# A ninth token block written to the two halves of one set of columns, and scaled on GpSimd with the even blocks

## The chip, the cores and the metric

The kernel runs on one core of a Trainium2 chip: TensorE (PE, with its weight loads PEld), VectorE (DVE), ScalarE (ACT), GpSimd (POOL), SyncE (SP, which issues DMAs), and DMA engines. The metric is the device time of one execution in microseconds (us), lower is better. Three runs of the kernel before gave 999.74, 1000.41 and 995.54 us, median 999.74.

## The reference

Attention with a threshold, and behind it a mixture of experts that sends each token to one expert. Cut to what is computed:

```python
# q, k, v: (8 sequences, 8 heads, 576 tokens, 64) f32
scores = scale * q @ k.T
scores = where(scores >= max(scores) - tau, scores, -1e9)
attn = exp(scores - max(scores)); attn /= sum(attn) + 1e-9
x = (attn @ v), heads side by side            # (4608 tokens, 512)
logits = x @ w_gate; e = argmax(logits)       # 8 experts
gate = softmax(logits)[e]; eom = sigmoid(x @ w_output_gate)[e]
out = gate * eom * (relu(x @ w1[e]) @ w2[e])  # w1: 512 x 1024, w2: 1024 x 512
```

## The kernel before

**Units.** Two sequences are worked on together, one in the partitions 0 to 63, one in 64 to 127. A unit is one head of such a pair: 4 pairs x 8 heads = 32 units. A sequence of 576 tokens is four blocks of 128 tokens and a rest of 64; with two sequences that is nine blocks of 128 rows, the ninth holding the 64 last tokens of both.

**Steps.** `Attention.run` goes through the units in five steps each (t = 0 to 4), with one order written out by hand for PE, DVE, ACT and POOL. In a step PE computes the scores of block t (L128) into PSUM tiles ps, DVE reduces them to their least negative (L137, tile s), POOL makes the threshold from that (thr, L142), ACT takes the exponential (L149), and in the next step DVE applies the mask and sums (L159). Two steps after the scores PE transposes the block: the remainder, 64 keys, in L177 into the banks pr and pa, the rest in L190 into pt; ACT copies both out into PTa and PTb (L181 and L192). pt is one buffer: L190 of the next step writes it again only when ACT has copied it. Attention times v (L221) of the unit before runs in between, and leaves X, 64 features of each sequence by 576 tokens.

**x_rows and what follows it.** In step 4 `x_rows` (L243 to L252) turns X of the unit before into rows of tokens, and gives the logits with them: wx is an identity of 64 columns beside 16 gate columns, so each matmul gives 80 columns. Sequence 0 goes to the bank pr, sequence 1 to pa, five blocks each. A matmul in f32 is two passes, so there are ten passes for each sequence. ACT copies pa and pr to xl (L314), with the remainder's copies (L181) in between, since they share the banks. Then `x_out` scales by the reciprocal of the sums: POOL the blocks of 128 tokens (L262), ACT the ninth block, one half from each sequence (L264). POOL scales the logits (L271). Behind that, in step 0 of the next unit, ACT copies pt to PTb (L192).

**Ninth block in before.** The fifth matmul of both sequences is 128 columns wide: sequence 0 takes its tokens from 512 and 64 columns of zeros, sequence 1 its tokens from 448, so that the last 64 land in the lower half. Each sequence has its own columns in xl, reciprocals and logits (10 of them), and the router copies the lower half of the logits of sequence 1 into one common block (L483).

**Router and experts.** After eight units the logits of a pair are summed (L282), routed and the rows scattered to DRAM by POOL (L456); the expert stage, from about 519 us on, is matmuls of 128 rows and 128 columns (L928 to L952), with weights loaded by SP and split on ACT and DVE.

Of the kernel before, what the change touches and what calls it, by code (L numbers as in the profile page):

```python
# [8 lines left out]
F32 = mybir.dt.float32  # L9
# [3 lines left out]
AF = mybir.ActivationFunctionType  # L13
ALU = mybir.AluOpType
AX = mybir.AxisListType
PSUM = bass.MemoryType.PSUM
P = 128
# [4 lines left out]
class Attention:  # L22
# [9 lines left out]
    def __init__(self, ctx, tc, ident, qkv, tau, wg, shape, router):  # L32
        self.tc, self.nc = tc, tc.nc
        nc = self.nc
        self.qkv = qkv
        self.B, self.H, self.S, self.D = shape
        self.NB = self.S // P
        self.M = self.NB * P
        self.R = self.S - self.M
        self.HS = self.S // 2  # L40
        self.KP = self.S + self.R
        self.QA = 2 * P
        self.NK = 2 * self.NB + 1
        self.nu = self.B // 2 * self.H
        self.router = router
        pool = lambda name, bufs, **kw: ctx.enter_context(tc.tile_pool(name=name, bufs=bufs, **kw))
        self.ld = pool("ald", self.LB)
        self.sp = pool("asp", 3)
        self.const = pool("aconst", 1)
        self.vld = pool("avld", self.VB)  # L50
        self.w2 = pool("aw2", 1)
        self.w3 = pool("aw3", 3)
        self.xp = pool("axp", 1)
        self.ps_s = pool("ps_s", 2, space=PSUM)
        self.ps_t = pool("ps_t", 1, space=PSUM)
        self.ps_a = pool("ps_a", 1, space=PSUM)
        self.ps_r = pool("ps_r", 1, space=PSUM)
        c = self.const
        self.ident = ident
        self.tau = c.tile([P, 1], F32, name="tau_sb")  # L60
        self.tau_in, self.wg_in = tau, wg
        warm = c.tile([P, 1], F32, name="warm")
        nc.vector.memset(warm, 0.0)
        nc.scalar.activation(warm, warm, AF.Exp)
        E2 = wg.shape[2]
        self.XW = self.D + E2
        self.wx = c.tile([P, self.H, self.XW], F32, name="wx")
        self.X = [c.tile([P, self.S + 64], F32, name=f"X{i}") for i in range(2)]
        self.half = [slice(0, 64), slice(64, P)]
        for pp in self.half:  # L70
            nc.gpsimd.tensor_copy(
                self.wx[pp, :, 0 : self.D], ident[pp, None, pp].broadcast_to([self.D, self.H, self.D])
            )
        for x in self.X:
            nc.gpsimd.memset(x[0:64, self.S :], 0.0)
        self.loaded, self.sums, self.rinv, self.lt, self.sumup = {}, {}, {}, {}, None

    def load_qk(self, u, first=False):
# [73 lines left out]
    def masks(self, u, t, ss, mn, thr, p, between=None):  # L152
        nc, S = self.nc, self.S
        if t == 0:
            self.sums[u] = self.w3.tile([P, 10], F32, name="sums")
        sums = self.sums[u]
        for a, s in enumerate(ss):
            e = p[:, a * S : a * S + S]
            nc.vector.scalar_tensor_tensor(  # L159
                e, s, thr[:, a : a + 1], e, op0=ALU.is_le, op1=ALU.mult, accum_out=sums[:, 2 * t + a : 2 * t + a + 1]  # L160
            )
            if a == 0 and between:
                between()
# [61 lines left out]
                yield (lambda: nc.scalar.copy(X[:, q0 : q0 + N], pa[:, 0:N])) if i == self.NB else None  # L225

    def denominators(self, u):
        r = self.rinv[u] = self.w3.tile([P, 10], F32, name="rinv")
        s = self.sums.pop(u)
        self.nc.gpsimd.tensor_scalar(r[:, 0:9], s[:, 0:9], 1e-9, None, op0=ALU.add)  # L230
        self.nc.gpsimd.tensor_copy(r[:, 9:10], r[:, 8:9])

    def inverse(self, u):
        r = self.rinv[u]
# [8 lines left out]
    def x_rows(self, u):  # L243
        X, pp, W, h = self.X[u % 2], self.half, self.XW, u % self.H
        ps = [pool.tile([P, 512], F32, name=name) for pool, name in ((self.ps_r, "pr"), (self.ps_a, "pa"))]
        for j in range(self.NB + 1):
            for a in range(2):
                c0 = self.M - 64 * a if j == self.NB else j * P
                self.nc.tensor.matmul(
                    ps[a][:, j * W : j * W + W], X[pp[a], c0 : c0 + P], self.wx[pp[a], h], start=True, stop=True  # L250
                )
        return ps  # L252

    def x_out(self, u, xl):
        nc, r, pp, D = self.nc, self.rinv[u], self.half, self.D
        bp, h = divmod(u, self.H)
        R = self.rows(bp)
        hs = slice(h * D, h * D + D)
        ra = r.rearrange("p (j a) -> p a j", a=2)
        for a in (1, 0):  # L260
            o = R[:, 0:8, hs].rearrange("p (j a) d -> p a j d", a=2)[:, a]
            nc.gpsimd.tensor_tensor(o, xl[:, a, 0:4, 0:D], ra[:, a, 0:4, None].broadcast_to([P, 4, D]), op=ALU.mult)  # L262
        for a in (1, 0):
            nc.scalar.activation(R[pp[a], 8, hs], xl[pp[a], a, 4, 0:D], AF.Copy, scale=r[pp[a], 8:9])  # L264

    def logits(self, u, xl):
        rt, r, E2 = self.router, self.rinv.pop(u), self.XW - self.D
        bp, h = divmod(u, self.H)
        if h == 0:
            self.lt[bp] = rt.small.tile([P, 10, E2, self.H], F32, name="ltx")  # L270
        self.nc.gpsimd.tensor_tensor(  # L271
            self.lt[bp][:, :, :, h].rearrange("p (j a) c -> p a j c", a=2), xl[:, :, :, self.D :],
            r.rearrange("p (j a) -> p a j", a=2)[:, :, :, None].broadcast_to([P, 2, 5, E2]), op=ALU.mult,
        )
        if h == self.H - 1:
            self.sumup = bp, rt.small.tile([P, 10, E2], F32, name="LX", bufs=2)

    def logit_sums(self, k):
        rt = self.router
        bp, LX = self.sumup  # L280
        ks = slice((0, 3, 6, 8)[k], (3, 6, 8, 10)[k])
        self.nc.vector.tensor_reduce(LX[:, ks], self.lt[bp][:, ks], axis=AX.X, op=ALU.add)  # L282
        if k == 3:
            self.lt.pop(bp)
            self.sumup = None
            rt.queue.append(rt.route(bp, rt.xrows[bp], LX))

    def run(self, hooks):
        nc, T, nu, rt = self.nc, self.NB + 1, self.nu, self.router
        G, W = nu * T, self.XW  # L290
        st, pr, av = {}, {}, {}
        self.prep_first()
        for g in range(G + T):
            u, t = divmod(g, T)
# [7 lines left out]
            if g < G:  # L302
                ps = [self.ps_s.tile([P, 1024], F32, name="ps") for _ in range(1 if t == self.NB and u else 2)]
# [3 lines left out]
            if xu is not None:  # L307
                px = self.x_rows(xu)
                out = self.remainder(t2, pr[g2], px) if rem else None
                if g < G:  # L310
                    pr[g] = self.exps(u, t, *st[g])
                xl = self.w2.tile([P, 2, 5, W], F32, name="xl")
                for a in (1, 0):
                    nc.scalar.copy(xl[:, a].rearrange("p j w -> p (j w)"), px[a][:, 0 : 5 * W])  # L314
                    if out:
                        out(a)
                self.x_out(xu, xl)
            elif g < G:
                pr[g] = self.exps(u, t, *st[g])
# [8 lines left out]
            if rem and xu is None:  # L328
                if not u:
                    self.pa = self.ps_a.tile([P, 512], F32, name="pa")  # L330
                out = self.remainder(t2, pr[g2], (self.ps_r.tile([P, 512], F32, name="pr"), self.pa), bool(u))
# [29 lines left out]
class Router:  # L361
# [109 lines left out]
    def route(self, bp, rows, LX):  # L471
        nc, E = self.nc, self.E
# [6 lines left out]
        cand, oh, t1, d = (t3(x) for x in ("cand", "oh", "t1", "d"))  # L479
        ohb = t3("ohb", BF16)  # L480
        V = nc.vector
        yield False
        nc.scalar.copy(LX[64:P, 8], LX[64:P, 9])  # L483
        yield True
        l, og = LX[:, 0:n, 0:E], LX[:, 0:n, E:]
        V.tensor_reduce(mx, l, axis=AX.X, op=ALU.max)
# [183 lines left out]
class Experts:  # L670
# [17 lines left out]
    def pool(self, name, bufs, **kw):  # L688
        return self.ctx.enter_context(self.tc.tile_pool(name=name, bufs=bufs, reuse_waits="tile", **kw))
# [460 lines left out]
```

## Time and profile before

| what | value |
|---|---|
| median of three runs | 999.74 us |
| the profiled execution, its own time | 1000.44 us |
| its span from first to last instruction | 998.4 us |
| PE busy | 963.6 us (97%) |
| DVE busy | 672.6 us (67%) |
| ACT busy | 631.6 us (63%) |
| POOL busy | 326.0 us (33%) |
| attention stage | to about 519 us |

The busy share of PE counts modelled ends of pipelined matmuls, so a short wait of PE can be partly hidden in it; from the start of one group of instructions to the start of the next nothing is hidden. Shapes such as 64*128 in a row of PE are the rows and columns of the array that the instruction uses.

### The profile page before, as it was taken

The page shows a single profiled execution, that of the slowest core. Times are in us where ns is not written, and L with a number is a line of the kernel's source. Part 1 is how long each engine was busy: PE and PEld are TensorE (multiplying, and loading weights), DVE is VectorE, ACT ScalarE, POOL GpSimd, SP SyncE. Part 2 cuts the span into 40 slices and gives each one's busy share as a digit, 9 for nine tenths or more (in the row PEclk, how much of TensorE's full clock was granted, in tenths as well). Part 3 has the DMA queues.
Part 4 walks back from the last instruction along what each step waited for, and adds up shares of the span by engine and source line. Part 5 has one row for each costly group of instructions (what it writes and reads, how often), then busy time and mean ns, then how long its engine had stood idle before and what let it go on. Part 6 is the DMA issues. An engine that isn't in the chain of part 4 may idle for free. (4 is left out here: it accounts for less than half of the span.)

```text
span 998.4 us, 21641 instructions
## 1 busy us (share of the span) xinstructions
PE 963.6 (97%) x8201; PEld 694.0 (70%) x8201; DVE 672.6 (67%) x1607; ACT 631.6 (63%) x1249; POOL 326.0 (33%) x617
## 2 busy tenths in 40 slices
PE   8999999999999999999989989999999999999994
PEld 4656566665666656666558878788878878878783
DVE  7888889888898888988865754435535535536621
ACT  6898888888889898898983333324424424425510
POOL 4344343458434584356625402012002102002101
PEclk9999999999999999999999999999999999999997
DMA  9972122123212233122227854345626426537301
GB/s 272 260 257 81 41 80 60 62 81 126 91 55 67 80 127 91 43 79 94 76 76 241 235 171 148 113 137 167 212 83 231 163 91 224 161 129 238 108 0 43
DMA packets 68841, 127.16 MB, mean 127 GB/s; under 512 B 6143, under 2 KB 32895, under 8 KB 68736
## 3 DMA queue, kind: packets, MB, share of 16 engines
q1 hardware_dynamic: 62096, 104.75, 33.7%
q0 software_dynamic: 6640, 21.02, 5.6%
q8 instruction: 65, 1.06, 0.4%
q14 instruction: 40, 0.33, 0.1%
HBM read 96.31 MB, written 30.22 MB: 127 GB/s over the span
## 5 line engine op out<-in xcount | busy, mean ns | idle before, releaser
L137 DVE TENSOR_SCALAR_CACHE_REDUCE s<-ps 128x576 f32<-128x576 f32 x288 | 207.4, 753 | 69.6 <-PE ps L128 68.8
L149 ACT ACTIVATE p<-s,mn 128x576 f32<-128x576 f32 x288 | 210.6, 774 | 60.4 <-DVE s L137 58.9
L159 DVE SCALAR_TENSOR_TENSOR p<-s,thr,p 128x576 f32<-128x576 f32 x288 | 224.9, 814 | 0.0
L128 PE MATMUL ps<-qk 64*128 64x288 f32 (+1 forms) x1152 | 194.4, 419 | 0.0
L142 POOL TENSOR_SCALAR thr<-mn,tau_sb 128x2 f32<-128x2 f32 (+1 forms) x160 | 117.5, 734 | 227.1 <-DVE s L137 224.8
L933 ACT ACTIVATE hh<-ph 128x512 fp32r<-128x512 f32 (+2 forms) x96 | 48.9, 510 | 208.1 <-PE ph L930 200.0
L934 DVE SCALAR_TENSOR_TENSOR hl<-ph,hh 128x512 fp32r<-128x512 f32 (+2 forms) x96 | 55.4, 577 | 142.7 <-ACT hh L933 142.6
L928 PE MATMUL ph<-xh,w1h 128*128 128x512 f32 (+2 forms) x384 | 136.5, 356 | 0.9 <-ACT xl L314 0.9
L929 PE MATMUL ph<-xl,w1h 128*128 128x512 f32 (+2 forms) x384 | 133.9, 349 | 0.2 <-DVE xl L755 0.2
L930 PE MATMUL ph<-xh,w1l 128*128 128x512 f32 (+2 forms) x384 | 133.7, 348 | 0.0
L128 PEld LDWEIGHTS ps<-qk 64*128 64x128 f32 (+1 forms) x1152 | 111.6, 189 | 21.2 <-DVE s L137 1.9
L952 PE MATMUL py<-w2h,hl 128*128 128x512 f32 x304 | 120.9, 398 | 4.5 <-DVE hl L934 4.5
L743 POOL DMA_INDIRECT out_dram<-yo,kid x39 | 44.0, 1129 | 236.8 <-DVE yo L742 87.6
L950 PE MATMUL py<-w2h,hh 128*128 128x512 f32 x304 | 120.3, 396 | 1.0 <-ACT hh L933 1.0
L951 PE MATMUL py<-w2l,hh 128*128 128x512 f32 x304 | 120.2, 395 | 0.0
L221 PE MATMUL pa<-PTb,vld 128*64 128x320 f32 x640 | 102.1, 447 | 0.7 <-ACT PTb L206 0.7
L190 PE MATMUL pt<-ident,p 64*128 64x64 f32 x2048 | 86.6, 224 | 8.1 <-ACT PTb L192 7.9
L221 PE MATMUL pa<-PTa,vld 128*64 128x256 f32 x640 | 83.2, 389 | 0.8 <-ACT PTb L181 0.8
L190 PEld LDWEIGHTS pt<-ident,p 64*128 64x128 f32 x2048 | 74.1, 139 | 12.6 <-ACT PTb L192 12.2
L755 DVE TENSOR_TENSOR w1l<-r,w1h 128x1024 fp32r<-128x1024 f32 x52 | 63.6, 1223 | 26.2 <-ACT w1h L752 25.3
L928 PEld LDWEIGHTS ph<-xh,w1h 128*128 128x128 f32 x384 | 72.6, 189 | 12.2 <-ACT xl L314 1.1
L929 PEld LDWEIGHTS ph<-xl,w1h 128*128 128x128 f32 x384 | 72.7, 189 | 10.2 <-DVE xl L755 0.6
(201 smaller groups left out, 1515.8 us busy)
## 6 DMA issues: line engine op xcount, KB each, us to landing
r<-in_moe_w_dram SPq DMA_DIRECT2D x104, 512.0 KB, 3.9
qk<-in_qkv_dram SPq DMA_DIRECT2D x31, 640.0 KB, 4.0
vld<-in_qkv_dram SPq DMA_DIRECT2D x32, 320.0 KB
xs<-zrow SPq DMA_DIRECT2D x32, 257.0 KB, 8.8
xg<-xs SPq DMA_DIRECT2D x6, 1028.0 KB, 5.3
xg<-xs SPq DMA_DIRECT2D x4, 514.0 KB
xg<-xs SPq DMA_DIRECT2D x2, 771.0 KB
out_dram<-yo,kid POOLq DMA_INDIRECT x39
```

The source lines that it names most:

```text
L128: nc.tensor.matmul(ps[a][:, c0 + hf * HS : c0 + hf * HS + HS], qs[pp], k[pp, k0 + hf * HS : k0 + hf * HS + HS], start=True, stop=True,)
L137: nc.vector.tensor_scalar(s, ps[a][:, c0 : c0 + S], SC, None, op0=ALU.mult, op1=ALU.min, accum_out=mn[:, a : a + 1])
L149: self.nc.scalar.activation(e, s, AF.Exp, bias=mn[:, a : a + 1], scale=-1.0)
L159: nc.vector.scalar_tensor_tensor(e, s, thr[:, a : a + 1], e, op0=ALU.is_le, op1=ALU.mult, accum_out=sums[:, 2 * t + a : 2 * t + a + 1])
L190: nc.tensor.transpose(pt[:, o : o + 64], p[hs[h], k0 : k0 + P], id_[hs[h], hs[h]])
L221: nc.tensor.matmul(pa[self.half[a], 0:N], vm[:, kb, a], PT[:, 4 * a + kb if i else self.NK - 1], start=(i == 0), stop=(i == self.NB), skip ...
L928: nc.tensor.matmul(ph, w1h[:, c, fs], self.xh[:, c, 0:N], start=(c == 0), stop=False)
L929: nc.tensor.matmul(ph, w1h[:, c, fs], self.xl[:, c, 0:N], start=False, stop=False)
L930: nc.tensor.matmul(ph, w1l[:, c, fs], self.xh[:, c, 0:N], start=False, stop=(c == 3))
L950: nc.tensor.matmul(Y, hh[:, ts], wh, start=(f == 0), stop=False)
L951: nc.tensor.matmul(Y, hh[:, ts], wl, start=False, stop=False)
L952: nc.tensor.matmul(Y, hl[:, ts], wh, start=False, stop=(f == 7))
```

## The change

The ninth block's two matmuls take 64 columns of X each as the stationary side, and write the two halves of the partitions of one set of 80 columns, both in pr. So xl, the reciprocals, the logits and their sums have nine blocks instead of ten in two groups; pa is copied with four blocks and pr with five, into every second place of xl. POOL scales the even blocks, now with the ninth, and the odd blocks; the two scaled copies on ACT, the copy of the ninth reciprocal on POOL, the copy in the router and the zero columns of X are gone.

```diff
-        self.X = [c.tile([P, self.S + 64], F32, name=f"X{i}") for i in range(2)]
+        self.X = [c.tile([P, self.S], F32, name=f"X{i}") for i in range(2)]
...
-        for x in self.X:
-            nc.gpsimd.memset(x[0:64, self.S :], 0.0)
...
-        self.nc.gpsimd.tensor_scalar(r[:, 0:9], s[:, 0:9], 1e-9, None, op0=ALU.add)
-        self.nc.gpsimd.tensor_copy(r[:, 9:10], r[:, 8:9])
+        self.nc.gpsimd.tensor_scalar(r, s, 1e-9, None, op0=ALU.add)
...
-                c0 = self.M - 64 * a if j == self.NB else j * P
+                last = j == self.NB
+                out = ps[0][pp[a], j * W : j * W + W] if last else ps[a][:, j * W : j * W + W]
                 self.nc.tensor.matmul(
-                    ps[a][:, j * W : j * W + W], X[pp[a], c0 : c0 + P], self.wx[pp[a], h], start=True, stop=True
+                    out, X[pp[a], j * P : j * P + (64 if last else P)], self.wx[pp[a], h], start=True, stop=True
                 )
...
         for a in (1, 0):
-            o = R[:, 0:8, hs].rearrange("p (j a) d -> p a j d", a=2)[:, a]
-            nc.gpsimd.tensor_tensor(o, xl[:, a, 0:4, 0:D], ra[:, a, 0:4, None].broadcast_to([P, 4, D]), op=ALU.mult)
-        for a in (1, 0):
-            nc.scalar.activation(R[pp[a], 8, hs], xl[pp[a], a, 4, 0:D], AF.Copy, scale=r[pp[a], 8:9])
+            nc.gpsimd.tensor_tensor(
+                R[:, a::2, hs], xl[:, a::2, 0:D], r[:, a::2, None].broadcast_to([P, 5 - a, D]), op=ALU.mult
+            )
...
-        ks = slice((0, 3, 6, 8)[k], (3, 6, 8, 10)[k])
+        ks = slice((0, 3, 5, 7)[k], (3, 5, 7, 9)[k])
...
-                xl = self.w2.tile([P, 2, 5, W], F32, name="xl")
+                xl = self.w2.tile([P, 9, W], F32, name="xl")
                 for a in (1, 0):
-                    nc.scalar.copy(xl[:, a].rearrange("p j w -> p (j w)"), px[a][:, 0 : 5 * W])
+                    nc.scalar.copy(xl[:, a::2], px[a][:, 0 : (5 - a) * W].rearrange("p (j w) -> p j w", w=W))
...
-        yield False
-        nc.scalar.copy(LX[64:P, 8], LX[64:P, 9])
```

PE's order at the end of x_rows in step 4 of a unit, before (pr and pa are the two banks, X_215 one of two buffers of X):

```order
L249 MATMUL pr<-wx,X_215 128x80
L249 MATMUL pa<-wx,X_215 128x80
L249 MATMUL pr<-wx,X_215 128x80
L249 MATMUL pa<-wx,X_215 128x80
L177 MATMUL pr<-ident,p 128x64
L177 MATMUL pa<-ident,p 128x64
L190 MATMUL pt<-ident,p 128x64 x16
L128 MATMUL ps<-qk 128x288 x4
```

And now:

```order
L247 MATMUL pr<-wx,X_215 128x80
L247 MATMUL pa<-wx,X_215 128x80
L247 MATMUL pr<-wx,X_215 64x80 x2
L175 MATMUL pr<-ident,p 128x64
L175 MATMUL pa<-ident,p 128x64
L188 MATMUL pt<-ident,p 128x64 x16
L126 MATMUL ps<-qk 128x288 x4
```

The last pair writes 64 partitions each of pr, and pa gets four blocks; the order around it is the same (the line numbers are two lower).

ACT's order from the last exponential of step 4 into step 0 of the next unit, before:

```order
L149 ACTIVATE p<-s,mn 128x576
L314 COPY xl<-pa 128x400
L181 COPY PTb<-pa 128x64
L314 COPY xl<-pr 128x400
L181 COPY PTb<-pr 128x64
L264 ACTIVATE rows<-xl,rinv 64x64 x2
L192 COPY PTb<-pt 128x8x128
L149 ACTIVATE p<-s,mn 128x576 x2
```

And now:

```order
L147 ACTIVATE p<-s,mn 128x576
L309 COPY xl<-pa 128x4x80
L179 COPY PTb<-pa 128x64
L309 COPY xl<-pr 128x5x80
L179 COPY PTb<-pr 128x64
L190 COPY PTb<-pt 128x8x128
L147 ACTIVATE p<-s,mn 128x576 x2
```

The two scaled copies between the remainder's copy and the copy of pt are gone, and the copy of pa has four blocks.

## Rows read from the trace of the kernel before

**Rows 1.** The page's busy times, share of the span, instructions.

```profile
PE 963.6 (97%) x8201; PEld 694.0 (70%) x8201; DVE 672.6 (67%) x1607; ACT 631.6 (63%) x1249; POOL 326.0 (33%) x617
```

**Rows 2.** Stretches: length, busy PE, PEld, DVE, ACT, POOL, PEclk, DMA, GB/s.

```profile
100.00:160.00 60.00, 59.32 (x684) 37.12 (x682) 52.39 (x147) 52.80 (x115) 23.89 (x38) 1.00 0.21 65
700.00:800.00 100.00, 100.00 (x561) 82.67 (x560) 50.38 (x63) 40.62 (x62) 11.00 (x14) 1.00 0.52 170
```

**Rows 3.** Waits of PE, 31 to 506 us: total us, times, longest.

```profile
PE pt L190 <- ACT PTb L192: 7.1, 30, 0.5
```

**Rows 4.** Timeline of PE in one unit: start, us, engine, line, operation.

```profile
331.54 0.27 PE L249 MATMUL pr<-wx,X 64*128 64x80 f32 x1
...
331.65 0.22 PE L177 MATMUL pr<-ident,p 64*128 64x64 f32 x1
...
331.71 0.66 PE L190 MATMUL pt<-ident,p 64*128 64x64 f32 x16
332.21 1.19 PE L128 MATMUL ps<-qk 64*128 64x288 f32 x8
333.33 1.08 PE L221 MATMUL pa<-PTa,vld 128*64 128x256 f32 x8
334.34 0.27 PE L177 MATMUL pr<-ident,p 64*128 64x64 f32 x1
...
334.85 0.71 PE L190 MATMUL pt<-ident,p 64*128 64x64 f32 x16 [0.23 <-ACT PTb L192]
335.39 1.19 PE L128 MATMUL ps<-qk 64*128 64x288 f32 x8
336.51 1.52 PE L221 MATMUL pa<-PTa,vld 128*64 128x256 f32 x12
337.96 0.28 PE L200 MATMUL pt<-ident,p 64*128 64x64 f32 x2
...
340.80 0.27 PE L177 MATMUL pr<-ident,p 64*128 64x64 f32 x1
...
340.91 0.66 PE L190 MATMUL pt<-ident,p 64*128 64x64 f32 x16
...
342.53 1.84 PE L221 MATMUL pa<-PTb,vld 128*64 128x320 f32 x12
344.30 0.27 PE L177 MATMUL pr<-ident,p 64*128 64x64 f32 x1
```

**Rows 5.** Timeline of ACT, step 4 into step 0 of the same unit.

```profile
331.38 0.78 ACT L149 ACTIVATE p<-s,mn 128x576 f32<-128x576 f32 x1 [0.69 <-DVE s L137]
332.06 0.47 ACT L314 COPY xl<-pa 128x400 f32<-128x400 f32 x1
332.44 0.21 ACT L181 COPY PTb<-pa 128x64 f32<-128x64 f32 x1
...
333.18 0.72 ACT L264 ACTIVATE rows<-xl,rinv 64x64 f32<-64x64 f32 x2
333.80 0.99 ACT L192 COPY PTb<-pt 128x1024 f32<-128x1024 f32 x1
```

**Rows 6.** Timeline of POOL and DVE in the same steps.

```profile
332.62 1.25 POOL L262 TENSOR_TENSOR rows<-xl,rinv 128x256 f32<-128x256 f32 x2 [0.38 <-ACT xl L314]
333.83 0.48 POOL L271 TENSOR_TENSOR ltx<-xl,rinv 128x160 f32<-128x160 f32 x1
...
331.26 0.08 DVE L137 DVE_READ_ACCUMULATOR s<-ps 128x1 f32 x1
...
334.79 0.08 DVE L137 DVE_READ_ACCUMULATOR s<-ps 128x1 f32 x1
```

**Rows 7.** Timeline of PE and ACT at the end of the stage.

```profile
507.04 0.27 PE L177 MATMUL pr<-ident,p 64*128 64x64 f32 x1
...
508.16 0.71 PE L190 MATMUL pt<-ident,p 64*128 64x64 f32 x16 [0.85 <-ACT PTb L192]
...
507.12 0.99 ACT L192 COPY PTb<-pt 128x1024 f32<-128x1024 f32 x1
```

More of the change, by code (lines that the diff above doesn't have):

```diff
@@ L154, in masks @@
         if t == 0:
-            self.sums[u] = self.w3.tile([P, 10], F32, name="sums")
+            self.sums[u] = self.w3.tile([P, 9], F32, name="sums")
         sums = self.sums[u]
@@ L227, in denominators @@
     def denominators(self, u):
-        r = self.rinv[u] = self.w3.tile([P, 10], F32, name="rinv")
+        r = self.rinv[u] = self.w3.tile([P, 9], F32, name="rinv")
         s = self.sums.pop(u)
-        self.nc.gpsimd.tensor_scalar(r[:, 0:9], s[:, 0:9], 1e-9, None, op0=ALU.add)
-        self.nc.gpsimd.tensor_copy(r[:, 9:10], r[:, 8:9])
+        self.nc.gpsimd.tensor_scalar(r, s, 1e-9, None, op0=ALU.add)
     def inverse(self, u):
@@ L254, in x_out @@
     def x_out(self, u, xl):
-        nc, r, pp, D = self.nc, self.rinv[u], self.half, self.D
+        nc, r, D = self.nc, self.rinv[u], self.D
         bp, h = divmod(u, self.H)
@@ L258, in x_out @@
         hs = slice(h * D, h * D + D)
-        ra = r.rearrange("p (j a) -> p a j", a=2)
         for a in (1, 0):
-            o = R[:, 0:8, hs].rearrange("p (j a) d -> p a j d", a=2)[:, a]
-            nc.gpsimd.tensor_tensor(o, xl[:, a, 0:4, 0:D], ra[:, a, 0:4, None].broadcast_to([P, 4, D]), op=ALU.mult)
-        for a in (1, 0):
-            nc.scalar.activation(R[pp[a], 8, hs], xl[pp[a], a, 4, 0:D], AF.Copy, scale=r[pp[a], 8:9])
+            nc.gpsimd.tensor_tensor(
+                R[:, a::2, hs], xl[:, a::2, 0:D], r[:, a::2, None].broadcast_to([P, 5 - a, D]), op=ALU.mult
+            )
     def logits(self, u, xl):
@@ L269, in logits @@
         if h == 0:
-            self.lt[bp] = rt.small.tile([P, 10, E2, self.H], F32, name="ltx")
+            self.lt[bp] = rt.small.tile([P, 9, E2, self.H], F32, name="ltx")
         self.nc.gpsimd.tensor_tensor(
-            self.lt[bp][:, :, :, h].rearrange("p (j a) c -> p a j c", a=2), xl[:, :, :, self.D :],
-            r.rearrange("p (j a) -> p a j", a=2)[:, :, :, None].broadcast_to([P, 2, 5, E2]), op=ALU.mult,
+            self.lt[bp][:, :, :, h], xl[:, :, self.D :], r[:, :, None].broadcast_to([P, 9, E2]), op=ALU.mult
         )
         if h == self.H - 1:
-            self.sumup = bp, rt.small.tile([P, 10, E2], F32, name="LX", bufs=2)
+            self.sumup = bp, rt.small.tile([P, 9, E2], F32, name="LX", bufs=2)
     def logit_sums(self, k):
```

## The prediction

> **What bounds the kernel now.** I read the busy shares first. TensorE (PE) is busy for 97% of the span and no other engine above 67% [rows 1]. The table by stage says where that holds: about 59.3 of 60 us in the attention stage, all 100 us in a stretch of the expert stage, both at the full granted clock [rows 2]. The change touches only the attention stage and its end, so what matters there is PE's remaining idle time, and whether a saved piece stays saved: the expert stage is PE back to back, so what attention ends earlier, the kernel ends earlier.
>
> Next the list of waits of PE. It has one item of size: the transposes of line 190 wait for ScalarE's (ACT's) copy PTb of line 192, 30 times between 31 and 506 us, 7.1 us in all [rows 3]. Ends of matmuls are modelled, so I read the true size in PE's timeline, from start to start [rows 4]. A unit (one head of a pair of sequences) has five steps. Step 4 ends with the last of ten x_rows passes at 331.54, its transposes at 331.65 and 331.71; step 0 is the scores at 332.21, L221 at 333.33, the remainder L177 at 334.34 and the transposes L190 at 334.85. From that L177 to L190 0.51 us go by; in step 3 the same pair takes 0.11 (340.80 to 340.91). Behind it the transposes take 0.54 (334.85 to 335.39) instead of 0.50 (331.71 to 332.21, where nothing was waited for). So PE loses 0.40 + 0.04 = 0.44 us in each unit, in step 0.
>
> What ends that wait is on ACT [rows 5]: copies of xl and the remainder from 332.06 on, then the two scaled copies of the ninth block (L264, 0.72 us at 333.18), and only then the PTb copy, from 333.80 to 334.79, 0.06 before PE goes on.
>
> **The change, part by part.**
>
> *ACT loses L264.* The PTb copy can start where L264 started: 333.80 − 333.18 = 0.62 us sooner. The first xl copy shrinks from 400 to 320 columns; 400 columns take 0.38 to the next start (332.06 to 332.44) [rows 5], so 80 fewer give at most 0.07. ACT is 0.69 us early and PE needs 0.44: the stall goes whole, with 0.25 to spare, more if PE itself comes later. Gain: 0.44 us a unit. The strided writing of xl moves as many elements as before; I cost it at nothing beside the 0.25.
>
> *PE's ninth block changes shape.* It is two passes for each sequence before and after. Before, each is a 64*128 tile, in pairs side by side, 0.11 apart (331.54 to 331.65, the last step) [rows 4]. After, the stationary part is 64 columns by 64 rows, both halves into the bank pr. No row shows a 64*64 tile, so I bound it by rows of other shapes. A pass streams its columns: twelve records (six pairs) of L221 take 1.45 at 256 columns (336.51 to 337.96) and 1.77 at 320 (342.53 to 344.30), so 64 columns cost 0.32/6 = 0.053, and 80 cost 0.067. At 0.11 apart, the x_rows passes are held by something beside streaming that a half-width stationary part should halve too. What is left of those groups is the cost of a change of tile shape: 1.45 − 6 × 0.213 = 0.17, 1.77 − 6 × 0.267 = 0.17, the eight records at 333.33 give 1.01 − 4 × 0.213 = 0.16, the eight of the scores at 332.21 give 1.12 − 4 × 0.24 = 0.16. Where the shape stays (331.65 to 331.71) the step is 0.06, where it has changed (340.80 to 340.91) 0.11. So 0.16 a change, and the ninth block adds two: into 64*64 and back to 64*128 for L177. Against 2 × 0.16 = 0.32 stand three steps (the pass before the block and its own two) at 0.067 instead of 0.11, −0.13. I take +0.19 us a unit. Lower bound, changes free: −0.13. Upper bound, each of the four passes alone with its own change: 4 × (0.067 + 0.16) = 0.91, the change back 0.16, less 0.04 and the 0.22 that the passes take now: +0.81. The value taken is the one that the rows of all three existing shapes agree on.
>
> The Trainium skill, page "TensorEngine Tiling (Array Packing)", section "Tiling Modes", says that changing the tiling mode, not just the tile, drains TensorE. The 0.16 at each change of shape agrees with it, and by it a change to 64*64 would cost the same; the trace has no such tile. The sum would be the one taken here.
>
> *GpSimd (POOL) gets the ninth block.* The multiplication of the even blocks grows from four to five blocks of 64: 1.25/2 = 0.63 us each at 332.62 [rows 6], so about +0.16; the logits lose a tenth of 0.48 and the copy of the ninth reciprocal goes. POOL's next duty in the unit is thr, which waits for VectorE (DVE) until 334.87 (334.79 + 0.08) [rows 6]; POOL's multiplications ended at 334.31 (333.83 + 0.48). 0.16 later is hidden with 0.4 to spare. Nobody but the scatter of line 456, a unit or more later, reads these rows.
>
> *DVE's reciprocals and logit sums* lose one of ten blocks, ACT loses one small copy for each pair, the route of the third pair moves one turn earlier, two memsets go before the first threshold. None of it stands before PE in rows 3: nothing.
>
> *What is late next.* With PE 0.44 earlier in step 0, the scores of step 1 would start 1.01 + 0.11 + 0.50 = 1.62 after L221's 333.33, at 334.95. They overwrite what DVE's second reduction reads until 334.87. The margin is 0.08; DVE hands over to ACT in about 0.04 (331.34 to 331.38 in rows 5 and 6). It just fits.
>
> *The end of the stage.* In the last step 0 there are no scores; L190 waits until 508.16, 1.12 after L177, for the PTb copy that began at 507.12 [rows 7]. There ACT sets the pace, so its 0.69 counts and PE's 0.19 mostly doesn't, but the last ninth block and POOL's longer multiplication lie on the way into the experts: I take +0.5 for this end.
>
> **The sum.** 30 units × (0.44 − 0.19) = 7.5, with the end 8.0 us. Against the profiled execution: 1000.44 − 8.0 = 992.4. That execution is 0.7 above the median of the runs, 999.74, so a median of 991.7.
>
> **The rivals.**
>
> 1. *The shape is free.* 0.44 + 0.13 = 0.57 a unit, 17.1 + 0.6: a median near 982. For it: the halves stay in the same rows. Against: every change between the three shapes in rows 4 costs the same 0.16. 7%.
>
> 2. *The halves don't run side by side.* The two halves write one bank; now they write pr and pa. If the streams follow each other, two passes cost 0.067 more each: 0.44 − 0.32 = 0.12 a unit, 3.6 + 0.5 = 4.1: 995.6. For it: in rows 4 all pairs of tiles that differ in rows (L177, with its pr and pa; x_rows) go to separate banks. Against: L221's two halves share pa and run 0.27 a pair. 14%.
>
> 3. *Slower.* One mechanism: in the ninth block every pass is kept apart from the one before it, by an emptying of the array as at a change of shape: the upper bound, +0.81 against 0.44. 30 × 0.37 = 11.1 us more, near 1011. It decides from +0.44 a unit on; that is between one emptying more than I count and two. For it: no row shows a row tile sharing a bank with another. Against: a pair in one bank is nothing new by columns. 10%. The same page, section "Restrictions and Gotchas", says that different row tiles cannot access one PSUM bank at the same time; that speaks for rivals 2 and 3, and this trace cannot test it.
>
> 4. *DVE takes the wait's place.* If the hand-over to step 1's scores takes more than the 0.08, or the longer GpSimd multiplication slows the reduction beside it, PE waits there. At 0.1 a unit the gain falls by 3: 994.7. Against: the scores of the other steps show no such wait in rows 3. 8%.
>
> **How the numbers follow.** My forecast, 991.7, has 61%; its own range is 989 to 994. The range of 8 in 10, 986.5 to 998.5, holds rivals 2 and 4 and leaves out 1 and 3. 0.5% of 999.74 is 5.0 us, about what a measurement of this kernel tells from no change. Faster by more than that is below 994.7: nearly all of the forecast, rival 1, half of rival 4 and little of 2, 0.67 after a shade for single runs (995.54 to 1000.41). Same: 0.21. Slower: 0.12.
>
> **What would show it.** In the changed profile the wait of L190 on PTb should be gone from PE's waits but for the end; from the remainder L177 of step 0 to the transposes 0.11; the units should follow each other 0.25 us closer than now. The ninth block should show 64*64 tiles, both halves within some ns, with about 0.16 before it and behind it. If each half starts 0.07 after the other it is rival 2, if 0.2 or more rival 3; if PE waits for s of L137 in step 1, rival 4. Units no closer than now with the stall gone would make the prediction wrong by the price of the shape; a stall that stays would make it wrong at its root.

## The result and the profile after

| | median us | runs | ratio to the kernel before |
|---|---|---|---|
| before | 1000.41 (995.54 to 1001.19) | 7 | 1 |
| after | 990.50 (989.46 to 992.15) | 7 | 0.9913 [0.9892, 0.9935] |

The forecast was 991.7, with a range of 986.5 to 998.5, and 989 to 994 for the likeliest case. The profiled execution after took 990.50 us; its span, from the first instruction to the last, is 988.7. The first lines to compare are those of the stretch in which the change acts. The busy times of the page after (engine, busy us, share of the span, instructions):

```profile
PE 963.6 (97%) x8201; PEld 693.0 (70%) x8201; DVE 672.2 (68%) x1607; ACT 615.8 (62%) x1181; POOL 315.5 (32%) x583
```

PE does what it did before, to 0.1 us [rows 1]; ACT has lost 16 us. What shrank is the span. The stretch of the attention stage after (columns as in [rows 2]):

```profile
100.00:160.00 60.00, 60.00 (x688) 37.45 (x686) 52.98 (x147) 51.99 (x108) 22.92 (x35) 1.00 0.22 67
```

PE is now busy for 60.00 of 60 us, where 59.32 stood before. The waits of PE from 31 to 506 us after (total us, times, longest):

```profile
PE pa L219 <- ACT PTb L204: 0.7, 1, 0.7
PE pa L219 <- ACT PTb L179: 0.2, 1, 0.2
```

The wait that was there 30 times [rows 3] is gone, and what is left are two single waits, both after 499 us, in the last unit. PE's timeline in the same steps of a unit after (start, us, engine, line, operation; L247 is the x_rows, L175 the remainder, L188 the transposes, L126 the scores, L219 the weighted sums; two rows in which pr and pa stand side by side are shown by their first):

```profile
327.71 0.27 PE L247 MATMUL pr<-wx,X 64*128 64x80 f32 x1
...
327.82 0.27 PE L247 MATMUL pr<-wx,X 64*128 64x80 f32 x1
...
328.03 0.36 PE L247 MATMUL pr<-wx,X 64*64 64x80 f32 x4
328.31 0.27 PE L175 MATMUL pr<-ident,p 64*128 64x64 f32 x1
...
328.43 0.66 PE L188 MATMUL pt<-ident,p 64*128 64x64 f32 x16
328.93 1.19 PE L126 MATMUL ps<-qk 64*128 64x288 f32 x8
330.05 1.08 PE L219 MATMUL pa<-PTa,vld 128*64 128x256 f32 x8
331.06 0.27 PE L175 MATMUL pr<-ident,p 64*128 64x64 f32 x1
...
331.17 0.66 PE L188 MATMUL pt<-ident,p 64*128 64x64 f32 x16
331.67 1.21 PE L126 MATMUL ps<-qk 64*128 64x288 f32 x8
332.81 1.52 PE L219 MATMUL pa<-PTa,vld 128*64 128x256 f32 x12
```

Two things are to be seen, against [rows 4]. In step 0 the transposes follow the remainder after 0.11 us (331.06 to 331.17, 0.51 before) and last 0.50 (0.54): the 0.44 is back. At the ninth block there is a new gap: the 64*64 passes begin 0.21 after the last 64*128 pass (327.82 to 328.03), 0.28 later the remainder begins and 0.12 after it the transposes. Before, the step from pass to pass was 0.11, and from the remainder to the transposes 0.06. From start to start over all units, the x_rows group took 1.338 us instead of 1.179 and the remainder behind it 0.111 instead of 0.056: 0.214, or 0.215 before rounding, is what the shape costs. The unit, the time from one x_rows group to the next, went from 15.701 to 15.480 (medians).

ACT, POOL and DVE in the same steps after (the same columns):

```profile
327.88 0.78 ACT L147 ACTIVATE p<-s,mn 128x576 f32<-128x576 f32 x1 [0.69 <-DVE s L135]
...
328.71 0.43 ACT L309 COPY xl<-pa 128x320 f32<-128x320 f32 x1
...
329.22 1.30 POOL L258 TENSOR_TENSOR rows<-xl,rinv 128x256 f32<-128x256 f32 x2 [0.47 <-ACT xl L309]
...
329.62 1.06 ACT L190 COPY PTb<-pt 128x1024 f32<-128x1024 f32 x1
...
330.48 0.46 POOL L267 TENSOR_TENSOR ltx<-xl,rinv 128x144 f32<-128x144 f32 x1
...
331.51 0.08 DVE L135 DVE_READ_ACCUMULATOR s<-ps 128x1 f32 x1
...
331.69 0.79 POOL L140 TENSOR_SCALAR thr<-mn,tau_sb 128x2 f32<-128x2 f32 x1 [0.19 <-DVE s L135]
```

The PTb copy L190 now stands right behind the copies of xl and of the remainder; POOL is done with its multiplications at 330.94 and waits for DVE again before thr.

### The profile page after: what moved, and what is told of

It reads as the page before. It is cut to its first block, busy times and chain, and to the rows that moved or that the text cites. A ratio compares the mean times of both kernels' runs of the same rounds, so it can differ in the third digit from the quotient of the medians.

```text
span 988.7 us, 21599 instructions
## 1 busy us (share of the span) xinstructions
PE 963.6 (97%) x8201; PEld 693.0 (70%) x8201; DVE 672.2 (68%) x1607; ACT 615.8 (62%) x1181; POOL 315.5 (32%) x583
## 5 line engine op out<-in xcount | busy, mean ns | idle before, releaser
L126 PE MATMUL ps<-qk 64*128 64x288 f32 (+1 forms) x1152 | 195.3, 421 | 0.0
L140 POOL TENSOR_SCALAR thr<-mn,tau_sb 128x2 f32<-128x2 f32 (+1 forms) x160 | 113.6, 710 | 229.6 <-DVE s L135 227.9
L126 PEld LDWEIGHTS ps<-qk 64*128 64x128 f32 (+1 forms) x1152 | 112.9, 189 | 20.4 <-DVE s L135 1.7
L219 PE MATMUL pa<-PTb,vld 128*64 128x320 f32 x640 | 102.4, 447 | 0.7 <-ACT PTb L204 0.7
L188 PE MATMUL pt<-ident,p 64*128 64x64 f32 x2048 | 85.1, 223 | 0.3
L219 PE MATMUL pa<-PTa,vld 128*64 128x256 f32 x640 | 83.2, 389 | 0.2 <-ACT PTb L179 0.2
L923 PEld LDWEIGHTS ph<-xh,w1l 128*128 128x128 f32 x384 | 72.2, 188 | 8.7
```

The source lines that it names most:

```text
L126: nc.tensor.matmul(ps[a][:, c0 + hf * HS : c0 + hf * HS + HS], qs[pp], k[pp, k0 + hf * HS : k0 + hf * HS + HS], start=True, stop=True,)
L140: self.router.gate = nc.gpsimd.tensor_scalar(thr[:, 0:n], mn[:, 0:n], self.tau, None, op0=ALU.add)
L219: nc.tensor.matmul(pa[self.half[a], 0:N], vm[:, kb, a], PT[:, 4 * a + kb if i else self.NK - 1], start=(i == 0), stop=(i == self.NB), skip ...
L923: nc.tensor.matmul(ph, w1l[:, c, fs], self.xh[:, c, 0:N], start=False, stop=(c == 3))
```

## The experiments

Times differ from chip to chip more than from run to run, so I read each experiment by its stretches: when the first x_rows group starts, the unit (median), from the first to the last x_rows group (31 steps), and what is left of the span. These columns are us of the profiled execution; the median is that of all executions of the kernel in its study. Rows without a ratio are one execution each. The chips of the study are called A, B and C.

| kernel | chip | first x_rows | unit | first to last | rest | span | median | ratio to before on that chip |
|---|---|---|---|---|---|---|---|---|
| before | | 31.39 | 15.701 | 484.77 | 482.25 | 998.4 | 1000.41 | 1 |
| after | | 32.33 | 15.480 | 476.97 | 479.42 | 988.7 | 990.50 | 0.9913 [0.9892, 0.9935] |
| b2_before_again | A | 31.50 | 15.707 | 484.89 | 481.72 | 998.1 | 1000.15 | |
| e1_gpsimd_only | A | 31.45 | 15.265 | 478.86 | 482.33 | 992.6 | 994.26 | 0.9943 [0.9932, 0.9955] |
| e2_layout_only | A | 32.01 | 15.793 | 487.20 | 481.13 | 1000.3 | 1000.75 | 1.0005 [0.9997, 1.0014] |
| e3_ninth_first | A | 32.15 | 15.330 | 472.51 | 480.31 | 985.0 | 986.64 | 0.9867 [0.9853, 0.9882] |
| e4_no_64x64 | B | 31.68 | 15.327 | 472.51 | 478.01 | 982.2 | 984.12 | 0.9895 [0.9878, 0.9911] |
| e5_ninth_unscaled | B | 31.05 | 15.264 | 470.45 | 476.45 | 978.0 | 979.67 | |
| e6_own_banks | B | 32.00 | 15.487 | 477.51 | 478.07 | 987.6 | 989.30 | |
| e7_memsets_kept | B | 31.92 | 15.477 | 476.84 | 477.74 | 986.5 | 988.21 | |
| e8_no_64x64_pa_first | C | 31.53 | 15.285 | 471.17 | 480.49 | 983.2 | 985.43 | 0.9856 [0.9835, 0.9877] |
| e9_after_again | C | 32.26 | 15.480 | 476.95 | 482.15 | 991.4 | 991.73 | 0.9914 [0.9898, 0.9931] |
| e10_before_again | C | 31.39 | 15.704 | 484.83 | 482.31 | 998.5 | 1000.62 | |

The kernel before took 999.86 on chip A, 994.68 on B and 999.97 on C (medians). My theory A: the unit is 15.70, less the stall of L190 (0.44), plus what the changes of shape cost (0.215). The rivals are in the expectations.

### e1_gpsimd_only: the kernel before, with only the scaling moved

```
-            nc.scalar.activation(R[pp[a], 8, hs], xl[pp[a], a, 4, 0:D], AF.Copy, scale=r[pp[a], 8:9])
+            nc.gpsimd.tensor_scalar(R[pp[a], 8, hs], xl[pp[a], a, 4, 0:D], r[pp[a], 8:9], None, op0=ALU.mult)
```

> The kernel before, with one thing changed: the two scaled copies of the ninth block go from ScalarE to GpSimd (two more multiplications of 64x64 there). The matmuls keep their one shape of 64*128 and their two banks. Theory A (the change gains the stall of 0.44 us a unit and pays about 0.21 for the 64*64 shape): the wait of the transposes on PTb goes, nothing is paid, the unit goes from 15.70 to about 15.28 us (0.02 for step 1's scores), 30 units and the end give 13 us: ratio to before about 0.987, some 3 to 4 us faster than the changed kernel. Rival B (the gain came from the smaller copy, the nine instead of ten blocks and the fewer instructions, the stall follows the layout): the unit stays above 15.6, ratio above 0.996.

Most units came as theory A has it, 15.26. But the median is 994.3, not 987: one unit took 19.61 us, one 17.88, and some 15.45 to 15.62. The long one in the timeline:

```profile
237.45 1.00 POOL L264 TENSOR_SCALAR rows<-xl,rinv 64x64 f32<-64x64 f32 x2 [3.05 <-DMA xs<-rows,dsti]
...
240.49 0.32 POOL L142 TENSOR_SCALAR thr<-mn,tau_sb 128x2 f32<-128x2 f32 x1
...
240.84 0.82 DVE L159 SCALAR_TENSOR_TENSOR p<-s,thr,p 128x576 f32<-128x576 f32 x1 [2.90 <-POOL thr L142]
...
242.47 0.27 PE L177 MATMUL pr<-ident,p 64*128 64x64 f32 x1 [1.71 <-DVE p L159]
```

POOL waits 3.05 us for an earlier scatter; thr L142 is queued behind the waiting instruction, DVE waits for thr, PE for DVE. POOL sat idle like this before the copies of the ninth block alone (2 of 64, 6.0 us in all), never before the multiplications of L262. In the same unit L262 carries waits for scatters too, but for those issued by 228.6 us, which had landed when it began its second half at 233.78; the copy behind it carries one for the scatter issued at 231.1. These scatters send the rows of the pair of sequences before, while the copy writes those of the present one; why it has to wait for them the trace doesn't tell. So the stall can be taken away without any change of shape, but this way hands a part of the gain to POOL's queue.

### e2_layout_only: the kernel after, with the scaling back on ACT

```
-                R[:, a::2, hs], xl[:, a::2, 0:D], r[:, a::2, None].broadcast_to([P, 5 - a, D]), op=ALU.mult
+                R[:, a:8:2, hs], xl[:, a:8:2, 0:D], r[:, a:8:2, None].broadcast_to([P, 4, D]), op=ALU.mult
+        for pp in (self.half[1], self.half[0]):
+            nc.scalar.activation(R[pp, 8, hs], xl[pp, 8, 0:D], AF.Copy, scale=r[pp, 8:9])
```

> The changed kernel, with one part undone: the ninth block is scaled on ScalarE again, in two halves of 64x64, at the place where they stood before; the layout, the 64*64 matmuls and the nine blocks stay. Theory A: the stall comes back as far as ScalarE's later copy reaches: 0.07 us sooner than before by the smaller copy of pa, against a TensorE that now comes 0.21 later, so some 0.15 of stall is left, the unit takes about 15.63, ratio to before 0.997 to 0.999. The price of the shape is then hidden under the stall. Rival B: the layout itself made the gain, the unit stays near 15.48, ratio near 0.991.

No gain: 1.0005, unit 15.793, 0.09 above before. I had let the shape's price disappear in the wait that is there anyway. The rows of ACT and PE show why it doesn't:

```profile
333.40 0.78 ACT L147 ACTIVATE p<-s,mn 128x576 f32<-128x576 f32 x1 [0.69 <-DVE s L135]
334.22 0.43 ACT L311 COPY xl<-pa 128x320 f32<-128x320 f32 x1
...
335.91 0.99 ACT L190 COPY PTb<-pt 128x1024 f32<-128x1024 f32 x1
```

```profile
336.57 0.27 PE L175 MATMUL pr<-ident,p 64*128 64x64 f32 x1
...
336.95 0.71 PE L188 MATMUL pt<-ident,p 64*128 64x64 f32 x16
```

The copies of xl wait for the x_rows: from the exponentials to the first copy it is 0.82 us now (333.40 to 334.22) against 0.68 before (331.38 to 332.06 in [rows 5]), because PE is done later with the ninth block and the remainder behind it. 0.05 of it comes back from the shorter copy, so the PTb copy starts 2.51 after the exponentials instead of 2.42, and these 0.09 are the unit's. The price lies ahead of the chain on ACT that ends in the stall; the wait still stands (0.38 in place of 0.11).

### e3_ninth_first: the 64*64 passes ahead of the 64*128 ones

```
-        for j in range(self.NB + 1):
+        for j in (self.NB, *range(self.NB)):
```

> The changed kernel, with the ninth block's 64*64 matmuls issued first of the x_rows passes instead of last. Before them stand scores of shape 128*128, so one change of shape there is needed in any case, and only one is added where the changed kernel adds two. Theory A: from the first x_rows pass to the transposes 1.29 us instead of 1.45, the unit about 15.32 instead of 15.48, 4 to 5 us faster than the changed kernel, ratio to before about 0.987. Rival C (the price of the ninth block is that both halves write one bank, not the changes of shape): the order changes nothing, unit 15.48, ratio 0.991.

It came as expected: 0.9867 [0.9853, 0.9882], unit 15.330, the x_rows group 1.241 instead of 1.338. The last x_rows pass and what follows it:

```profile
325.07 0.27 PE L247 MATMUL pr<-wx,X 64*128 64x80 f32 x1
...
325.18 0.22 PE L175 MATMUL pr<-ident,p 64*128 64x64 f32 x1
...
325.24 0.67 PE L188 MATMUL pt<-ident,p 64*128 64x64 f32 x16
```

The steps to L175 and L188 are 0.11 and 0.06 again, as in [rows 4]. Ahead of the x_rows stand scores of another shape (128*128), so a change of shape is paid there anyway; now the program has one more change than before, not two. Its price, 1.241 − 1.179 = 0.062, is 0.15 below that of the order in the kernel after.

### b2_before_again

> The kernel before, once more, for a second profile. In the first two profiles the first x_rows began 1.0 us later in the changed kernel, and what follows the attention stage was 2.9 us shorter. If the start and the expert stage vary by as much from one execution of one kernel to the next, this profile shows another start and another length of the expert stage with units of 15.70; if they belong to the change, it shows 31.4 us to the first x_rows and 482 us behind the last.

Units of 15.707, the first x_rows at 31.45: the kernel before is the same from run to run up to the end of attention.

### e4_no_64x64 and e8_no_64x64_pa_first: no change of shape, full height on GpSimd

Both keep the layout of xl and the scaling of the kernel after, and compute the ninth block as before. e4 against after:

```
+            nc.gpsimd.memset(x[0:64, self.S :], 0.0)
...
+                c0 = self.M - 64 * a if j == self.NB else j * P
...
-                    out, X[pp[a], j * P : j * P + (64 if last else P)], self.wx[pp[a], h], start=True, stop=True
+                    ps[a][:, j * W : j * W + W], X[pp[a], c0 : c0 + P], self.wx[pp[a], h], start=True, stop=True
...
+                nc.scalar.copy(xl[64:P, 8], px[1][64:P, 4 * W : 5 * W])
```

> The kernel after with the ninth block's two matmuls as 64*128 steps again (over X with its 64 added columns and their memset), each into its own bank; ScalarE copies the lower half of the ninth block of the second bank apart (one 64x80 copy, about 0.2 us) into the ninth place of xl, so that POOL still scales whole-partition tiles. Theory A (the unit's time is the stall, which is gone, plus the price of the 64*64 shape, 0.215 us in the kernel after): no change of shape is left, the x_rows group goes back from 1.338 to 1.18 us and the step to L175 from 0.111 to 0.056; the added 0.2 us of ScalarE fits into the 0.25 us that the kernel before had to spare, so the unit takes 15.26 to 15.28 us against 15.48 after and 15.327 with the ninth block first; the median 983.5 to 986. Rival (ScalarE's spare is smaller than that): the wait of L188 on L190's copy comes back by up to 0.2 us, unit 15.3 to 15.47, median 986 to 991.

0.9895 [0.9878, 0.9911], unit 15.327: no shape is paid (x_rows 1.178 and 0.056), no wait of the transposes came back (0.111), yet 0.06 is missing, and neither theory had its place. It is in the scores of step 0, 1.180 against 1.122. What the trace says of L221, the sums behind them: their engine sat idle until (us, times)

```profile
  ACT xl L313: 15.5, 32
```

and in one unit:

```profile
326.00 0.22 ACT L313 COPY xl<-pa 64x80 f32<-64x80 f32 x1
...
326.27 1.08 PE L221 MATMUL pa<-PTa,vld 128*64 128x256 f32 x8
```

The small copy is the last reader of the bank pa (until 326.22), and the sums write pa; in all units but the last they start 0.05 after its end. In e8 the two banks are exchanged, so that pa is read first:

```
-        ps = [pool.tile([P, 512], F32, name=name) for pool, name in ((self.ps_r, "pr"), (self.ps_a, "pa"))]
+        ps = [pool.tile([P, 512], F32, name=name) for pool, name in ((self.ps_a, "pa"), (self.ps_r, "pr"))]
...
-                for a in (1, 0):
+                for a in (0, 1):
```

> The kernel e4 with the banks of the two sequences exchanged: the first sequence's rows go to the bank pa, the second's to pr, and ScalarE copies pa whole first, so that the 64x80 copy that comes last reads pr. In e4 the unit was 15.327, 0.06 more than the 15.264 of the kernel without the scaled copies; the scores of step 0 took 1.180 there against 1.122, and the weighted sums L221 behind them began right as the 64x80 copy (the last reader of pa) ended. Theory A (that copy holds the bank): pa is free 0.4 us sooner, the scores of step 0 go back to about 1.12 and the unit to 15.265 to 15.29; 1.2 to 1.9 us less than e4 on one chip, ratio to before 0.987 to 0.988. Rival (ScalarE's added 0.2 us itself is what is late): unit 15.32 to 15.33 again, ratio 0.989 to 0.990.

```profile
325.04 0.22 ACT L313 COPY xl<-pr 64x80 f32<-64x80 f32 x1
...
325.26 1.08 PE L221 MATMUL pa<-PTa,vld 128*64 128x256 f32 x8
```

The copy reads pr now, and the sums start up to 0.015 before it ends: they no longer wait for it. (The view of L221's waits names the copy in e8 too, 10.8 us in 28 times; it puts a wait down to what ended last beside it, so the name alone does not settle it.) The scores of step 0 take 1.121 and the unit 15.285. 0.02 is left in the transposes of step 0 (0.518 for 0.497). The ratio, 0.9856 [0.9835, 0.9877], is a little better than expected; by the unit it is the best version that computes everything, 0.045 a unit under e3, though the ratios of the two overlap.

### e5_ninth_unscaled: what the scaled copies cost

The kernel before without L264; the scaled values of the ninth block are left out, its place is zero.

> The kernel before without its two scaled copies L264; row block 8 is set to zero once for each pair of units, so the scaled values of the ninth block are left out of the result. Theory A: the stall of L190 goes whole and no shape changes, so every unit takes 15.26 to 15.28 us, with no unit over 15.4; the median about 985 to 988 beside 1000 of the kernel before. This is what the copies' move to GpSimd alone should have given; if the units are even here, the long units there came from GpSimd's own waits. Rival (the long units come from the released stall itself, which lets ScalarE and TensorE run into the next wait): some units over 17 us here too, and a median of about 993.

The 27 full units without the routing's extra matmuls take 15.26 to 15.30, the three with them 15.52; none is long. The stall goes whole and nothing comes behind it. So the long units of e1 were GpSimd's waits, and 15.264 is what each version can be measured by: before +0.437, after +0.216, e3 +0.07, e4 +0.06, e8 +0.02.

### e6_own_banks: is it the shape or the shared bank?

```
-                out = ps[0][pp[a], j * W : j * W + W] if last else ps[a][:, j * W : j * W + W]
+                out = ps[a][pp[a], j * W : j * W + W] if last else ps[a][:, j * W : j * W + W]
```

> The kernel after with the ninth block's halves each in its own bank (columns 320 to 399 of pr and of pa, 64*64 shape kept), and a copy of 64x80 for each half on ScalarE. Theory A (the price is the change of shape): the first 64*64 step still starts 0.20 to 0.21 us after the last 64*128 one, and L175 0.16 us after the second, the x_rows group stays 1.33 to 1.34. Rival (the price comes of two row tiles writing one bank): the entry falls to about 0.11 us and the group to about 1.18. ScalarE has about 0.3 us more to do before L190, so a part of the wait of L188 may come back: that is told by the gap before L188 in step 0, apart from the group.

ScalarE copies each half apart, two copies of 64x80 more in a unit (cut from the edit shown). The wait of the transposes stays away all the same (0.111 from L175 to L188 in step 0). PE's timeline at the ninth block:

```profile
327.60 0.27 PE L247 MATMUL pr<-wx,X 64*128 64x80 f32 x1
...
327.80 0.28 PE L247 MATMUL pr<-wx,X 64*64 64x80 f32 x1
327.81 0.28 PE L247 MATMUL pa<-wx,X 64*64 64x80 f32 x1
327.92 0.23 PE L247 MATMUL pr<-wx,X 64*64 64x80 f32 x1
327.93 0.23 PE L247 MATMUL pa<-wx,X 64*64 64x80 f32 x1
328.09 0.27 PE L175 MATMUL pr<-ident,p 64*128 64x64 f32 x1
```

The steps are 0.20 into the block, 0.12 inside it and 0.17 out of it, and the group takes 1.338. Over all units the medians are the same as in the kernel after (0.208, 0.120, 0.167), where both halves write one bank. It is the shape. The halves start 0.01 apart here and 7 ns apart there: rivals 2 and 3 are answered.

### e7_memsets_kept: the start

```
+        self.X = [c.tile([P, self.S + 64], F32, name=f"X{i}") for i in range(2)]
...
+        for x in self.X:
+            nc.gpsimd.memset(x[0:64, self.S :], 0.0)
```

> The kernel after with X's 64 added columns and their two memsets on GpSimd kept, not used by any matmul. Nothing of the attention changes: unit 15.48. The question is the start, where the first x_rows group came at 31.39 us before and at 32.40 after, and the full clock was granted at 4.9 and 7.2 us. Theory M (the memsets' place in the start decides when the clock rises): first x_rows at 31.4 to 31.5, full clock by 5.3 us. Rival N (chance, or where the program lies): 32.2 to 32.4 again, full clock at 6 to 7.3 us.

The first x_rows came at 31.92, outside both expected ranges, beside 32.00 (e6, without the memsets) and 31.05 (e5, built like before) on the same chip: the memsets are not it.

### e9_after_again and e10_before_again: one chip, both profiles

> The kernel after once more, unchanged, on one chip with a profile of the kernel before (next run). By the profiles so far the change is worth 7.2 us from the first to the last x_rows group and 0.6 in the last unit, and costs about 0.9 at the start, wherever it runs; the 2.9 us after the last x_rows group that the first pair showed are not the change's. If so, the pair on one chip differs by 6.0 to 7.5 us of span (ratio 0.993 to 0.994) where both have the same number of half-clock stretches. Rival (the expert stage gains too): 9 to 10 us, and the rest after the last x_rows group 2.5 to 3 us shorter than before's.

> The kernel before unchanged, for a profile on the chip of the run above: first x_rows at 31.0 to 31.5, unit 15.70, last unit 12.36. The rest after the last x_rows group is what is asked: 477.5 to 478.5 (then the kernel before is at about 994.5 here and the change worth 6 to 7 us), or 481 to 482.5 (then about 1000).

The x_rows on PE in before (e10) and after (e9): minimum, median and maximum ns, then the first and the last start:

```profile
L249 PE MATMUL pr<-wx,X x320: 272/272/333, 31.4 to 517.2; 64*128 64x80 f32 x160
```

```profile
L247 PE MATMUL pr<-wx,X x384: 229/272/333, 32.3 to 510.4; 64*128 64x80 f32 x128, 64*64 64x80 f32 x64
```

The spans differ by 7.2 us: +0.9 to the first x_rows, −7.9 from there to the last, −0.2 behind. The 2.8 that the first pair differed by behind the last x_rows do not come with the change each time. The same 4 us of the kernel after in the first profile and in e9 (columns as in [rows 2]):

```profile
567.00:571.00 4.00, 4.00 (x22) 3.60 (x21) 2.31 (x4) 1.43 (x2) 0.00 (x0) 1.00 0.78 268
```

```profile
567.00:571.00 4.00, 4.00 (x15) 3.81 (x14) 1.89 (x4) 0.00 (x0) 0.00 (x0) 0.58 0.68 200
```

In e9 the granted clock is at its lower level for 3.4 us there, PE gets 15 matmuls done instead of 22, and the same program ends 2.6 us later; 1.5 of them arise in this stretch (e9 is 0.8 late where it begins and 2.3 where it ends). In the 7 us up to it PE was busy for 5.1 us in both executions. The kernel before has one such stretch in each of its three profiles, the kernel after none in its first and one in e9. The medians of this chip are 8.2 us apart, those of the first pair 9.9; the ratios agree (0.9914 and 0.9913).

## Why the prediction was right, step by step

**The stall.** Right in place and size: 0.44 a unit, whole, in step 0. e5 alone shows it: 15.264, where the three profiles of the kernel before have 15.701 to 15.707.

**The shape.** Right in kind, 0.215 instead of 0.19, and the sum came near because its parts erred in both directions. I had counted three steps at 0.067 and a change of 0.16 before and behind the block: 0.227, 0.067, 0.227. Measured were 0.208, 0.120 and 0.167, and then 0.111 for the 0.056 from L175 to L188. The 0.11 behind a change of shape had been read from the rows (340.80 to 340.91), but it was left out of the sum. The step that failed is "a half-width stationary part should halve" what holds the passes: the two passes of the block are 0.12 apart, no quicker than 64*128 ones. The change into the block adds 0.096 to the step of 0.112 that was there, the change out of it 0.055 + 0.055. A change is not free, so rival 1 is out. The 0.16 read from rows where the shape changes between streams was in the right size, but it isn't a constant to be added to the streaming. The Trainium skill, page "TensorEngine Tiling (Array Packing)", section "Tiling Modes", says that changing the mode drains TensorE; the 0.21 into the block agrees, in one bank or two (e6).

**One bank for both halves.** They run side by side, 7 ns apart. The same page's section "Restrictions and Gotchas" lets different row tiles not access one PSUM bank at the same time; here two tiles that differ in rows and columns start 7 ns apart in one bank, and keep the pace that they have in two (e6). Rivals 2 and 3 are out.

**POOL.** Its multiplication for the sequence with five blocks grew from a mean of 0.64 to 0.73 us (0.16 more was forecast), and is hidden. What I didn't see is that the layout does POOL a service that e1 lacks: the ninth block goes into the multiplication of the even blocks, and in the kernel after POOL never sat idle for a scatter before it.

**What is late next.** The forecast margin of 0.08 before the scores of step 1 is in the rows: DVE is done with the second reduction at 331.59, the scores start at 331.67. They take 0.02 longer than before (1.140 for 1.119), so rival 4 exists at a fifth of its price. e5, without the longer multiplication on POOL, has 1.140 too, so it is the hand-over.

**The end of the stage.** Forecast +0.5; the last unit went from 12.36 to 11.76. The step 0 in it waits 0.42 from L175 to L188 instead of 1.12:

```profile
500.88 0.27 PE L175 MATMUL pr<-ident,p 64*128 64x64 f32 x1
...
501.30 0.71 PE L188 MATMUL pt<-ident,p 64*128 64x64 f32 x16
```

**The sum.** 30 × 0.25 + 0.5 = 8.0 was forecast; measured are 7.2 over the 30 units and 0.6 at the end, 7.8. The 7.2 are 30 times 0.22, or 6.6, and 0.6 more: ten units of the kernel before were longer than the median, up to 15.94, against three after, at 15.74. The forecast has no term for these. In e5, which keeps the router's work as it was, all units together are 0.9 over 30 times the median (1.4 before, 0.8 after), so most of it, too, comes from the two copies. Two further terms were not foreseen. The start costs 0.9, in each profile of the kernel after. In the first pair 2.8 fell away behind the attention stage. About 1.6 of it is a stretch at the lower clock (0.50 from 578.4 to 581.8 us before), which the execution after didn't meet; ahead of it, from 559 us on, PE waits for ACT and DVE at other matmuls in one kernel than in the other, and the cause of that remainder stays open. So 9.7 of span in the first pair was −7.8, +0.9 and −2.8; on chip C, with one stretch at the lower clock in each execution, it was 7.2. That the forecast came so near the median is partly luck, because these two terms had opposite signs; the mechanism carries 7 to 8 us of it.

## What to carry to other kernels

A busy share of 97% with one wait repeated in every unit is worth a look at what the waited-for engine does just ahead, and the price must be put on the right side of the chain: what delays the chain's start (e2) isn't absorbed by the wait at its end. A matmul tile of another shape costs a change into it and one out of it (0.21 us here), so put it next to a place where the shape changes anyway (e3, 0.06). When work goes to another engine, ask what its instruction waits for that the old one didn't, and who is queued behind it (e1); and which bank a small copy keeps from its next writer (e4).

## What the runs showed of the hardware that I had not expected

The start. The kernels with the layout of after reach their first x_rows 0.14 to 0.95 us later than those built like before on the same chip (31.53 to 32.33 against 31.05 to 31.50). The first eight passes of the scores in before (e10) and after (e9):

```profile
4.38 1.49 PE L128 MATMUL ps<-qk 64*128 64x288 f32 x8
```

```profile
4.38 2.29 PE L126 MATMUL ps<-qk 64*128 64x288 f32 x8
```

They begin at the same time and wait for nothing that the profile shows, and PE had run the same seven passes of the warm-up up to there, in 3.17 us in both. The trace's record of the granted clock begins with the higher level (2.4 GHz) at 4.9 us in before and at 7.1 in after; the 512-column passes of the warm-up start 0.43 us apart ahead of it and 0.22 behind it. Over all 13 profiles the order is the same without exception: the later that rise, from 4.2 us (e5) to 7.2 (the first profile of after), the later the first x_rows, from 31.05 to 32.33. It isn't the memsets (e7); why the rise comes later stays open.

Small stationary parts. 64*64 passes of 80 columns follow each other at 0.12 us, 64*128 ones at 0.11 (e6): a smaller part isn't quicker.

The chips. The part behind the attention stage took 476.5 to 478.1 us on chip B and 480.3 to 482.3 on A and C, whatever was changed ahead of it. That would be most of the 5 us by which the kernel before differs there; it was not profiled on B.
